# Causal block attention and channel mix on one core: one start-up write moved to ScalarE, and all 1033 tasks in another order

## The chip, the core and the metric

The kernel runs on one core of a Trainium2 chip. The core has five engines that work side by side, each on its own queue of instructions and each strictly in the order of that queue: TensorE (PE, with weight loads shown apart as PEld), VectorE (DVE), ScalarE (ACT), GpSimd (POOL) and SyncE (SP), which here issues every DMA. Engines wait for each other through semaphores. The metric is the device time of one execution in microseconds.

## What is computed

The inputs are q, k and v of 8 batches with 8 heads, 576 positions and 64 numbers per head, and the weights of a channel mix. Attention is causal by blocks of 64 positions:

```python
scores = scale * np.matmul(q, k.transpose(0, 1, 3, 2))
mask = block_i >= block_j                      # position // 64
attn = softmax(np.where(mask, scores, -1e9))
x = np.matmul(attn, v)                         # heads side by side: 512 channels
x_prev = shift of x by one position, zero in front
xk = mu_k * x + (1.0 - mu_k) * x_prev
xr = mu_r * x + (1.0 - mu_r) * x_prev
k = np.maximum(xk @ w_k, 0.0)
v = k * k @ w_v
out = sigmoid(xr @ w_r) * v
```

(The softmax and the shift are written here as words; the rest is the reference.)

## The kernel before

**Tasks and orders.** The kernel first lists its work as 1033 tasks, numbered from 0 in the order in which they are added. Each has a function that issues its instructions, the engines that may do it, and the buffers that it uses from small rings. Nothing is scheduled while it runs: `ORDER` (lines 17 to 72) is a written list of task numbers, and the tasks are issued in that sequence (lines 885 and 886), so the part of the list that falls to one engine is that engine's queue. A word such as `123+1` is task 123 with one fill ahead of it: a matmul of the identity with a width of 512 whose result nobody reads (`unread`, line 257, the matmul is L259). `PLACE` has one letter for each task that more than one engine may do, in order of the numbers: A for ScalarE, D for VectorE, P for GpSimd. A buffer is taken from its ring when the first task that uses it is issued, and freed after the last.

**Stages of one batch.** For batches 0 to 3, long loads bring q and k (tag `ld`, line 234), casts to bfloat16 follow (`long`, L245 on ScalarE, L251 on VectorE and GpSimd), TensorE transposes them (`qt`, L313), and copies put them into `t_qkt` (`ev`). For batches 4 to 7 loads of another layout are cast (`qk`, `tail`) and SyncE transposes them by DMA (`turn`, L377). v is loaded by eight DMAs and cast (`v`). Scores are 12 tasks per batch, `sc b g i` for g of 0 and 1 and i of 0 to 5 (L484), each followed by an exponential on ScalarE, `ex b g i` (L493), which writes `t_e` from the score buffer `t_s` (three in its ring).

Attention outputs come from passes over `t_e`: for batches 1 to 7 an S pass for the row sums (L530, 60 matmuls), a T pass (16), and the value passes A and B (72 each, L541). Batch 0 is done in two parts of its own: positions 0 to 319 and 320 to 575. Each part has column sums (L639) and two value passes (L646). VectorE turns the sums, inverts them and multiplies (t1, rec, t2, norm), which fills columns 1 to 576 of `t_xt`. Column 0 of `t_xt` is the position ahead of the first, and stays zero.

**The mix.** For each of four channel groups a difference of neighbouring columns (`d`, L706, VectorE or GpSimd) and the two mixes (`mul`, L720, VectorE) write `XK` and `XR`. They are worked on in chunks of 512 positions: `pk` multiplies by w_k (L749), `relu` (L760, L762) and `sq` (L770, L772) follow, `pr` multiplies by w_r (L788) with a tanh behind it (L796), `pv` multiplies by w_v (L814), VectorE forms the output (`o`, L826) and SyncE stores it (`store`, L834). `t_mm`, where these products land, has two buffers.

**Task numbers that the text uses.** 100, 101 and 102 are the column sums and the two value passes of the second part of batch 0 (36, 72 and 72 matmuls). 123 and 127 are transposes of batch 1. 165 to 168 are the S, T, A and B passes of batch 1, and 519 to 522 those of batch 6. 543, 547, 551 and 555 are the loads of q and k of batch 7 for heads 0 to 3 and their partners (four DMA commands each); 546, 550, 554 and 558 are the DMA transposes of the same. 563 to 585 (odd) are the scores of batch 7. 966 and above belong to the last two chunks.

Of the kernel before, what the change touches and what calls it, by code (L numbers as in the profile page):

```python
# [11 lines left out]
AF = mybir.ActivationFunctionType  # L12
# [2 lines left out]
LONGS = 4  # L15

ORDER = """
3 0+12 5 4 6 10 7 8 9 11 12 15+8 17 24 16 13 14 18 61+3 63 64 62 19 25 20 21
22 55 57 58 23 56 26 27 28 65 66 29 30 67+1 68 69 70 71+4 33 34 59+2 31 60
32 1 125 72 79+2 82 77 78 81 73 74 83 80 84 85 87 75 126 86 2 127 97 99 121  # L20
76 91 92 122 100 103 98 88 39 41 93 40 123+1 133 124 104 42 134 89 90 94 95
101 102 106 105 107 43 96 108 44 118 115 117 35 116 128 141 119 36 45 46 147
148 143 625 626 129 130 120 142 631 109 632 633 200 112 135 658 136 110 628
659 113 145 629 630 627 37 38 131+1 132 643+4 644 646 144 146 647 648 151
152 649 137 640 645 650 163 164 155 156 652 641 642 651 653 654 655 656 657
153 154 637 638 616 161 162 159 617 201 639 634 635 636 160 139 114 610 611
202 613 203 188 157 140 149 150 158 614 615 660 661 189 190 49 618 111 191
619 612 47 48 138 620 621 50 165 53 166 169 170 168 54 51 622 623 662 52 624
672 196 197 171 172 175 173 198 185 663 192 193 199 673 186 664 194 330 195
167 187 174 228 208 229 176 675 178 177 209 665 676 206 218 216 219 204 222  # L30
669 670 217 223 210 179 343 674 214 215 666 181 211 182 183 180 230 667 231
184 220 221 212 681 699 213 682 224 225 275 226 700 671 693 694 683 227 205
677 678 267 268 207 695 232 679 680 233 236 237 239 238 240 234 241 684 685
686 344 243 271 247 244 696 697 276 277 278 702 272 345 253 698 263 703 245
235 687 264 265 688 689 266 337 701 331 246 704 705 335 690 269 691 692 242
273 274 248 254 257 706 279 710 707 280 270 297 349 250 255 298 711 299 300
256 716 717 258 281 249 259 289 283 336 290 295 708 718 284 296 346 719 709
720 712 293 294 301 303 304 261 302 743 744 745 740 741 291 287 305 288 742
722 723 251 474 737 332 738 713 731 292 714 739 407 732 341 339 306 715 333
285 286 252 725 724 726 728 733 307 282 729 308 311 309 340 312 746 334 747  # L40
668 314 408 338 313 315 734 730 342 748 749 727 310 316 324 398 411 347 735
317 359 736 360 721 262 355 325 413 326 405 750 760 751 761 356 318 367 368
369 319 409 371 320 370 752 753 260 763 764 372 357 348 358 363 364 321 762
757 373 374 351 758 365 352 322 327 328 401 410 790 791 485 754 755 323 366
361 353 362 403 399 778 779 404 329 769 781 770 771 766 350 767 354 375 400
376 379 782 783 380 792 780 382 787 381 793 788 768 789 784 785 383 786 377
412 417 418 765 384 378 385 772 773 389 402 775 776 406 429 421 422 774 423
424 777 390 759 386 387 794 430 414 795 804 805 487 488 391 431 432 439 427
796 388 797 807 395 440 479 397 808 428 806 798 425 799 756 392 426 437 438
433 834 835 393 396 475 801 394 802 816 817 435 434 441 436 419 825 826 810  # L50
420 415 442 416 542 480 446 543 483 811 818 444 476 443 447 448 450 812 449
453 477 451 836 831 478 827 837 459 832 489 481 490 482 484 461 486 460 813
814 815 828 829 553 803 830 819 822 462 820 823 824 557 551 821 445 452 838
839 463 833 842 843 844 464 454 467 501 497 517 498 455 458 502 518 465 456
545 840 468 851 809 457 841 852 503 800 469 507 508 499 500 845 495 544 504
472 491 509 848 846 849 493 878 496 511 880 510 552 879 881 470 549 875 876
555 860 854 492 512 877 513 514 494 547 861 505 515 855 850 856 466 872 857
506 546 516 519 873 858 520 874 548 521 869 870 871 866 867 859 863 523 524
525 868 526 864 865 556 527 522 528 529 862 886 887 558 882 883 530 532 554
579 580 531 583 584 471 550 847 473 573 574 884 885 895 853 581 582 539 541  # L60
567 568 577 578 559 892 896 897 560 893 540 889 894 890 569 565 563 533 922
564 923 561 536 534 537 924 925 919 916 920 917 570 566 538 904 905 921 585
562 575 571 906 901 576 902 586 903 913 914 915 572 926 918 927 587 891 588
590 591 898 899 900 592 593 594 595 910 911 535 907 908 597 607 909 601 888
912 589 596 936 937 928 939 929 608 603 609 938 940 602 933 934 930 931 966
967 941 968 969 970 604 971 598 935 932 599 605 942 948 943 945 949 606 950
951 946 947 944 952 953 954 955 956 960 961 962 957 958 600 1007 963 1008
964 965 1009 959 974 975 976 972 973 983 984 980 981 977 978 979 989 990 992
993 986 991 987 994 988 995 996 985 997 1004 1005 1006 1001 1002 998 999
1010 1011 1012 1013 1014 1015 1000 1003 1021 1022 1024 1025 1016 1017 982  # L70
1023 1030 1026 1031 1032 1018 1027 1019 1020 1028 1029
"""

PLACE = (
    "APAAPAADPPDDPPDDDPAAAAPADDDAPPPPPDPDAAPADDAADADPPDPAPAPADDADDDDPPAAA"
    "AAPAPDDPDDDPDPAPPDDDPDDDPDDPPAPAPPDDDPDPAPPADPDPPPPPDAAAAPPPADPPPPDA"
    "DADDDPAADPAPADAPDPDPDPDPDDDPDDAADPADAPAADPAADAADAAAPAAAPAAAPDPDDAPAD"
    "ADAAAPDAAADPAPDDAAAADAAAAADPDDDPDAAAAADPAAAAAPDDAAADDDDPDPAPADADAPAP"
    "ADADAAADADADAPAPADADAA")


class Plan:
# [53 lines left out]
def kernel(  # L136
# [12 lines left out]
    nc = tc.nc  # L149
# [4 lines left out]
    CCn = C // P  # L154
# [19 lines left out]
    for n, bufs in RINGS.items():  # L174
# [15 lines left out]
    slots = {(ring, at): pools[ring].tile(*SHAPES[ring], tag=f"{ring}{at}",  # L190
                                          name=f"t_{ring}{at}")
             for ring, n in RINGS.items() for at in range(n)}
# [6 lines left out]
    pick = consts.tile([P, 2, QC], F16)  # L199
# [14 lines left out]
            nc.vector.memset(pick[o * D:o * D + D, c,  # L214
                                  u * QC // 2:(u + 1) * QC // 2], 1.0)
    for n in range(RINGS["xt"]):
        nc.vector.memset(slots["xt", n][:, :, 0:1], 0.0)
    if LONGS < B:
        for n in range(RINGS["nl"]):
            nc.gpsimd.memset(slots["nl", n][D:P, :].rearrange(  # L220
# [661 lines left out]
    for (n, cc, a, z), t in mixed.items():  # L882
        t["deps"] += [r for lo, hi, r in readers[n]
                      if lo < z - RT and hi > a - RT]
    for t in plan.order():
        plan.issue(t)


# [28 lines left out]
```

## Time and profile before

| what | value |
|---|---|
| time of the kernel, median of 3 runs | 263.0 us (262.6 to 263.42) |
| the profiled execution, its own time | 261.88 us |
| its span, from the first to the last instruction | 260.1 us |
| mean granted TensorE clock in it | 0.986 |
| fills in the order | 38 |

The span is what the profile's views divide up; 1.78 us lie around it, and the profiled execution was 1.1 us shorter than the median. Times in the views count from the start of the span. A row of the timeline gives start, duration, engine, line, operation, what is written from what, and in brackets how long the engine sat idle before and what ended that. A row of the windows gives the stretch, its length, then busy time and number of instructions of TensorE, its weight loads, VectorE, ScalarE and GpSimd, the granted clock, the busy share of the DMA engines and GB/s. A row of the chain of waits gives start, duration and the piece of work that the end hung on. In the groups by line a row gives the group, its count, busy time, mean duration in ns, and the idle time before it.

### The profile page before, as it was taken

To read this page: it belongs to the slowest core of one execution; us is meant where nothing else is said; L and a number is where in the kernel's file an instruction comes from. 1 tells how busy PE (TensorE), PEld (TensorE's weight loads), DVE (VectorE), ACT (ScalarE), POOL (GpSimd) and SP (SyncE) were. 2 spreads that over 40 slices of the span, in tenths; PEclk is the share of its full clock that TensorE was granted. 3 is DMA by queue.
4 is the path that set the end of the run, shared out by engine and by line. 5 is a ranking of instruction groups with operands and counts; after the bars stand their busy time and mean duration, and the time that the engine had idled before them with its cause. 6 is when DMAs were issued, how large, how long until landed. Compare 5 with 4: busy or idle time off the path is not lost.

```text
span 260.1 us, 8110 instructions
## 1 busy us (share of the span) xinstructions
PE 244.3 (94%) x3434; PEld 124.5 (48%) x3434; DVE 185.4 (71%) x292; ACT 180.9 (70%) x246; POOL 84.6 (33%) x94
## 2 busy tenths in 40 slices
PE   7888379999999999989999999999999999999995
PEld 2545246665466444543554454435534454444442
DVE  0249586999879765796798979786885889543522
ACT  3599849978989998689649667799468840570630
POOL 4423325352255324131540065016351415230110
PEclk9999869999999999999999999999999999999999
DMA  7999999879867799979999899999885202201313
GB/s 224 277 262 359 325 204 312 272 185 222 281 204 176 178 223 226 184 163 229 220 172 260 184 200 159 290 207 226 120 214 156 98 3 81 83 1 40 121 40 124
DMA packets 110132, 48.77 MB, mean 188 GB/s; under 512 B 98704, under 2 KB 98960, under 8 KB 110096
## 3 DMA queue, kind: packets, MB, share of 16 engines
q1 hardware_dynamic: 110096, 48.25, 77.6%
q8 instruction: 27, 0.44, 0.7%
q14 instruction: 9, 0.07, 0.1%
HBM read 33.56 MB, written 9.44 MB: 165 GB/s over the span
## 4 chain that ended last, share of the span: by engine, by line
PE 79%; ACT 5%; DMA 5%; issue 3%; DVE 3%; SPq 2%; POOL 1%; POOLq 0%; ACTq 0%; DVEq 0%
PE t_mm L749 23%; PE t_mm L814 20%; PE t_mm L788 11%; PE t_s L484 7%; PE t_s L541 6%; PE t_s L530 4%; PE t_mm L259 3%; ACT t_e L493 3%; PE t_s L313 2%; SPq L234 2%; DMA t_qkt<-t_nl 2%; DMA t_ld<-in_k_dram 2%; DMA t_vl<-in_v_dram 1%; DVE t_xt L685 1%; PE t_s L646 1%
## 5 line engine op out<-in xcount | busy, mean ns | idle before, releaser
L493 ACT ACTIVATE t_e<-t_s 128x1024 f16<-128x1024 f32 (+3 forms) x96 | 87.7, 975 | 14.6 <-PE t_s L484 14.1
L749 PE MATMUL t_mm<-XK,WK 128*128 128x512 f16 (+2 forms) x320 | 69.6, 363 | 0.8 <-DVE t_o L826 0.6
L814 PE MATMUL t_mm<-WV,t_k 128*128 128x512 f16 (+1 forms) x296 | 66.9, 374 | 0.0
L772 POOL TENSOR_TENSOR t_k<-t_kr 128x512 f16<-128x512 f32 (+2 forms) x31 | 32.1, 1042 | 70.6 <-ACT t_kr L760 38.9
L749 PEld LDWEIGHTS <-WK 128*128 128x128 f16 x320 | 29.5, 99 | 33.4 <-issue 5.1
L826 DVE SCALAR_TENSOR_TENSOR t_o<-t_t,t_mm 128x512 f32<-128x512 f32 (+1 forms) x37 | 24.8, 671 | 28.2 <-PE t_mm L814 20.0
L760 ACT ACTIVATE t_kr<-t_mm 128x512 f32<-128x512 f32 (+2 forms) x50 | 29.1, 583 | 22.2 <-PE t_mm L749 21.6
L814 PEld LDWEIGHTS <-t_k 128*128 128x128 f16 x296 | 28.1, 98 | 33.8 <-issue 2.8
L796 ACT ACTIVATE t_t<-t_mm 128x512 f32<-128x512 f32 x36 | 21.7, 602 | 25.2 <-PE t_mm L788 25.2
L706 POOL TENSOR_TENSOR t_d<-t_xt 128x576 f32<-128x576 f32 (+2 forms) x20 | 21.7, 1091 | 50.6 <-DVE XR L720 19.1
L788 PE MATMUL t_mm<-WR,XR 128*128 128x512 f16 x144 | 36.4, 381 | 0.0
L484 PE MATMUL t_s<-t_qkt 64*64 64x64 bf16 (+7 forms) x672 | 29.7, 288 | 4.2 <-ACT t_e L493 1.4
L720 DVE SCALAR_TENSOR_TENSOR XR<-t_d,MUR,t_xt 128x576 f16<-128x576 f32 (+4 forms) x44 | 31.0, 711 | 0.2
L720 DVE SCALAR_TENSOR_TENSOR XK<-t_d,MUK,t_xt 128x576 f16<-128x576 f32 (+4 forms) x44 | 28.7, 675 | 0.6 <-POOL t_d L706 0.4
L251 POOL CAST t_nl<-t_ld 64x256 bf16<-64x256 f32 (+3 forms) x27 | 22.7, 849 | 16.8 <-DMA t_ld<-in_k_dram 10.2
L484 PEld LDWEIGHTS <-t_qkt 64*64 64x64 bf16 x672 | 14.7, 107 | 21.7 <-issue 16.1
L762 DVE TENSOR_SCALAR t_kr<-t_mm 128x512 f32<-128x512 f32 (+2 forms) x30 | 17.1, 577 | 10.7 <-PE t_mm L749 9.4
L541 PE MATMUL t_s<-t_e,t_vo 64*32 64x64 f16 (+7 forms) x1120 | 20.2, 284 | 0.3 <-POOL t_vo L251 0.3
L772 DVE TENSOR_TENSOR t_k<-t_kr 128x512 f16<-128x512 f32 (+2 forms) x23 | 15.4, 673 | 6.7 <-ACT t_kr L760 6.3
L788 PEld LDWEIGHTS <-XR 128*128 128x128 f16 x144 | 12.5, 98 | 15.4 <-issue 3.8
L541 PEld LDWEIGHTS <-t_vo 64*32 64x32 f16 x1120 | 14.5, 93 | 7.7 <-issue 2.5
L597 DVE TENSOR_TENSOR t_xt<-t_s,t_rt 128x1024 f32<-128x1024 f32 x14 | 16.9, 1218 | 0.7 <-PE t_s L541 0.6
(49 smaller groups left out, 188.6 us busy)
## 6 DMA issues: line engine op xcount, KB each, us to landing
t_vl<-in_v_dram SPq DMA_DIRECT2D x64, 144.0 KB, 3.7
out_dram<-t_o SPq DMA_DIRECT2D x35, 256.0 KB, 2.8
t_ld<-in_q_dram SPq DMA_DIRECT2D x16, 288.0 KB, 4.6
t_ld<-in_k_dram SPq DMA_DIRECT2D x16, 288.0 KB, 4.7
t_ld<-in_q_dram SPq DMA_DIRECT2D x36, 128.0 KB, 3.4
t_ld<-in_k_dram SPq DMA_DIRECT2D x36, 128.0 KB, 3.4
t_ld<-in_moe_w_k_dram SPq DMA_DIRECT2D x4, 512.0 KB, 7.0
t_ld<-in_moe_w_v_dram SPq DMA_DIRECT2D x4, 512.0 KB, 6.8
```

The source lines that it names most:

```text
L251: e.tensor_copy(dst, src)
L484: nc.tensor.matmul(PS[o * D:o * D + D, y, col:col + n], kq[:, 1, t * D:t * D + D], kq[:, 0, q0:q0 + n], start=True, stop=True)
L493: nc.scalar.activation(new(ebuf)[:, :, 0:w], new(m)[:, :, 0:w], AF.Exp, scale=ISQ)
L541: nc.tensor.matmul(PA[out_, u, HALF + f * D:HALF + f * D + D] if kind == "T" else PA[out_, u, lo - D:lo - D + n], weight(b, u, c, t % JT, ...
L706: (nc.vector if eng == "DVE" else nc.gpsimd).tensor_tensor(dt[:, lo:hi], x[:, cc, 1 + lo:1 + hi], x[:, cc, lo:hi], ALU.subtract)
L720: nc.vector.scalar_tensor_tensor((XK, XR)[n][:, cc, pos:pos + w], new(d)[:, at:at + w], (MUK1, MUR1)[n][:, cc:cc + 1], x, ALU.mult, ALU.add)
L749: nc.tensor.matmul(ps, WK[:, cc, jc * P:(jc + 1) * P], XK[:, cc, t0 % RT:t0 % RT + w], start=(cc == 0), stop=(cc == CCn - 1))
L760: nc.scalar.activation(kt, ps, AF.Relu)
L772: (nc.vector if eng == "DVE" else nc.gpsimd).tensor_tensor(dst, KR, KR, ALU.mult)
L788: nc.tensor.matmul(ps, XR[:, cc, t0 % RT:t0 % RT + P], WR[:, cc], start=(cc == 0), stop=(cc == CCn - 1))
L814: nc.tensor.matmul(ps[:, 0:w], k2[:, jc, jt * P:(jt + 1) * P], WV[:, jc, cols], start=(jc == 0), stop=(jc == JCn - 1))
L826: nc.vector.scalar_tensor_tensor(new(o)[:, 0:w], new(tiles["tbf", c, jt])[:, cols], 1.0, new(m)[:, 0:w], ALU.add, ALU.mult)
```

## The change

There are three edits. Column 0 of the two `t_xt` buffers is zeroed by ScalarE (a copy of part of `pick`, times 0) in place of VectorE, still ahead of all tasks; it is then the first operation of ScalarE. `ORDER` is another sequence of the same 1033 tasks, with 56 fills in place of 38, and `PLACE` gives some tasks to other engines. The loop that issues the tasks now notes what each one issued, with a condition that ends in `and 0`, so its dependency is never added. The computation is the same.

Of the two lists the rows are shown on which the text draws.

```diff
--- before
+++ after
 ORDER = """
-3 0+12 5 4 6 10 7 8 9 11 12 15+8 17 24 16 13 14 18 61+3 63 64 62 19 25 20 21
-22 55 57 58 23 56 26 27 28 65 66 29 30 67+1 68 69 70 71+4 33 34 59+2 31 60
...
-76 91 92 122 100 103 98 88 39 41 93 40 123+1 133 124 104 42 134 89 90 94 95
-101 102 106 105 107 43 96 108 44 118 115 117 35 116 128 141 119 36 45 46 147
...
-420 415 442 416 542 480 446 543 483 811 818 444 476 443 447 448 450 812 449
...
-814 815 828 829 553 803 830 819 822 462 820 823 824 557 551 821 445 452 838
...
-555 860 854 492 512 877 513 514 494 547 861 505 515 855 850 856 466 872 857
-506 546 516 519 873 858 520 874 548 521 869 870 871 866 867 859 863 523 524
-525 868 526 864 865 556 527 522 528 529 862 886 887 558 882 883 530 532 554
-579 580 531 583 584 471 550 847 473 573 574 884 885 895 853 581 582 539 541
...
-562 575 571 906 901 576 902 586 903 913 914 915 572 926 918 927 587 891 588
...
-1023 1030 1026 1031 1032 1018 1027 1019 1020 1028 1029
+3 0+12 5 4 8 9 6 10 17 19 18 12 7 24 25 11 13+9 15 16 14 59+5 60 63 57 26 20
...
+122 86 65 88 89 90 41 42 97 94 95 66 102+5 43 44 128 123+2 100+5 124 39 40
+45 103 98 104 35 622 96 36 101 623 145 99 141 129 130 624 146 46 37 105 625
...
+827 845 490 517 452 839 454 846 506 499 463 464 467 555 553 466 507 508 847
...
+864 865 880 881 551 495 494 496 511 515 471 860 861 862 866 872 873 512 516
+520 519 552 867 543 868 869 870 456 547 854 855 523 524 856 871 544 875 857
+850 526 858 525 522 529 521 874 528 554 876 877 527 557 558 533 859 892 893
+579 580 473 853 577 546 575 576 539 541 578 534 884 885 886 548 549 550 571
+569 894 585 572 586 559 895 844 887 540 570 888 924 535 583 896 925 573 581
...
+1026 1022 1023 1030 1031 1018 1032 1027 1019 1020 1028 1029...
 """
 PLACE = (
-    "APAAPAADPPDDPPDDDPAAAAPADDDAPPPPPDPDAAPADDAADADPPDPAPAPADDADDDDPPAAA"
...
+    "PDDDDADAPPADPDDDPDAAAPAPADAADPDDDDPDAAPAAADDDPDDPDPAPDPAPADADPDDPAAA"
...
     for n in range(RINGS["xt"]):
-        nc.vector.memset(slots["xt", n][:, :, 0:1], 0.0)
+        nc.scalar.activation(slots["xt", n][:, :, 0], pick[:, 0, 0:CCn],
+                             AF.Copy, scale=0.0)
...
+    shared = ("long", "qk", "tail", "v", "w", "d", "mul", "sq")
+    ahead = None
     for t in plan.order():
+        n0 = len(nc.cur_bb.bb.instructions)
         plan.issue(t)
+        made = nc.cur_bb.bb.instructions[n0:]
+        if t["eng"] == "DVE" and t["key"].split()[0] in shared:
+            ahead = made[-1]
+        elif t["eng"] == "POOL" and ahead is not None and 0:
+            tc.add_manual_dep(
+                made[0], ahead.name, mybir.DependencyInfo(
+                    mybir.DependencyClass.Sync,
+                    mybir.DependencyReason.DATA), reason="turns")
```

Read from the letters and the lists, the tasks move between engines like this (before, after):

| task | ScalarE | VectorE | GpSimd |
|---|---|---|---|
| squares | 26, 27 | 23, 28 | 31, 25 |
| relu | 50, 52 | 30, 28 | |
| differences | | 16, 22 | 20, 14 |
| casts of q and k (long, qk, tail) | 15, 16 | 10, 13 | 27, 23 |
| casts of v | 3, 1 | 8, 6 | 5, 9 |
| casts of weights | 6, 7 | 3, 1 | 1, 2 |
| copies of transposes | 13, 12 | 7, 8 | |

## What was predicted

> **What bounds the kernel now.** I read the page first: busy time, granted clock, and the chain that ended last.
>
> ```profile
> PE 244.3 (94%) x3434; PEld 124.5 (48%) x3434; DVE 185.4 (71%) x292; ACT 180.9 (70%) x246; POOL 84.6 (33%) x94
> PEclk9999869999999999999999999999999999999999
> PE 79%; ACT 5%; DMA 5%; issue 3%; DVE 3%; SPq 2%; POOL 1%; POOLq 0%; ACTq 0%; DVEq 0%
> ```
>
> TensorE is busy in 94% of the span of 260.1 us. A new order can win only the other 15.8 us (260.1 - 244.3) and the time lost at a lower clock, and the clock row dips in one place alone, near 30 us. So next I read the waits of TensorE and the timeline there.
>
> ```profile
> PE t_s L646 <- issue: 4.8, 2, 4.0
> 26.50 1.54 PEld L646 LDWEIGHTS <-t_vo 64*32 64x32 f16 x128 [1.09 <-issue]
> 26.50 1.70 PE L646 MATMUL t_s<-t_e,t_vo 64*32 64x256 f16 x128 [0.81 <-issue]
> 32.15 0.23 PE L646 MATMUL t_s<-t_e,t_vo 64*32 64x64 f16 x1 [3.95 <-issue]
> 34.28 1.07 PE L484 MATMUL t_s<-t_qkt 64*64 64x384 bf16 x12 [1.33 <-DVE t_xt L685]
> q8 instruction: 27, 0.44, 0.7%
> ```
>
> In the value passes of batch 0 TensorE stops twice for "issue": 0.81 us, then 3.95 us. Between the stops lie exactly 128 matmuls and 128 weight loads, 256 instructions. The instruction queue q8 moved 27 packets, 0.44 MB / 27 = 16 KB each, and 6868 TensorE instructions / 27 = 254. So I read both stops as TensorE waiting for its next block of 256 instructions. It took those 256 in 1.70 us, and the next block could run only 32.15 - 26.50 = 5.65 us after the start of the one before. After that comes a wait of 1.33 us for VectorE, itself late by the stop, and the clock:
>
> ```profile
> 30.00:31.00 1.00, 0.00 (x0) 0.00 (x0) 0.00 (x0) 1.00 (x2) 0.00 (x0) 0.86 0.98 364
> 32.00:34.00 2.00, 0.81 (x5) 0.28 (x6) 1.53 (x3) 0.00 (x0) 0.75 (x1) 0.50 0.93 269
> 34.00:36.00 2.00, 1.72 (x15) 0.85 (x15) 1.84 (x5) 0.98 (x2) 0.47 (x2) 0.50 1.22 185
> 36.00:37.00 1.00, 1.00 (x5) 0.60 (x4) 0.43 (x2) 0.95 (x2) 0.34 (x1) 0.50 0.90 176
> 37.00:38.00 1.00, 1.00 (x13) 0.77 (x12) 1.00 (x3) 0.37 (x1) 0.00 (x0) 0.73 0.98 184
> ```
>
> The clock is halved to about 37.5 us. TensorE was busy 0.81 + 1.72 + 1.00 + 0.54 = 4.1 us of that time, so about half, 2.0 us, was lost. Without the block stops TensorE would gain at most 0.81 + 3.95 + 1.33 + 2.0 = 8.1 us.
>
> But another engine stands close behind. I cut the span at the first exponential of batch 0 (11.76) and the last of batch 1 (51.51).
>
> ```profile
> 11.76:51.51 39.75, 31.55 (x627) 19.99 (x629) 29.25 (x58) 33.91 (x40) 13.60 (x18) 0.91 0.98 286
> 51.51:257.00 205.49, 203.14 (x2758) 100.03 (x2750) 154.60 (x227) 142.43 (x201) 65.19 (x60) 1.00 0.74 165
> 35.02 1.94 ACT L493 ACTIVATE t_e<-t_s 128x1024 f16<-128x1024 f32 x2 [3.53 <-PE t_s L484]
> 37.63 0.44 ACT L760 ACTIVATE t_kr<-t_mm 128x320 f32<-128x320 f32 x1 [0.68 <-PE t_mm L749]
> ```
>
> In the first stretch ScalarE is the fuller one: 33.91 us busy against TensorE's 31.55. It is idle for 5.84 us there, and 3.53 + 0.68 = 4.21 us of these are the stop seen from ScalarE. After 51.51 TensorE sits idle for 205.49 - 203.14 = 2.35 us only, so little is left to win.
>
> **The change, part by part.** *The block stops.* Before, the two value passes of the second part of batch 0 (tasks 101 and 102, 72 matmuls each) stand next to each other. In the new order 77 matmuls of task 102 (5 of them fills) are followed by 11 (2 fills), 41 (5 fills) and 4 others before 101. I cut the new TensorE stream into the same blocks.
>
> ```profile
> 23.04 1.15 PE L639 MATMUL t_mm<-t_e,pick 128*32 128x256 f16 x36
> 40.20 0.50 PE t_s L313 x9
> 48.12 0.54 PE t_mm L749 x4
> ```
>
> One edge falls after matmul 56 of task 102, the next after matmul 51 of task 101: 21 + 11 + 41 + 4 + 51 = 128. That is 72 value matmuls at 1.70 / 128 = 0.013 (1.0 us), nine transposes (0.5), 36 column sums (1.15), four of L749 (0.54) and seven fills at 0.24 (1.7, row below): 4.9 us in place of 1.70. The block before it comes to 4.5 us in the same way. Against the 5.65 us above, stops of 1.1 and 0.8 us remain. I take these 1.9 us, of which 0.9 us reaches ScalarE through the transposes of batch 1 behind the first; bounds are 0 and the old 4.76 us (0.81 + 3.95). When the clock fell, TensorE had been idle from 28.20 (32.15 - 3.95) to about 30.7 (the 0.86 of the row at 30), 2.5 us; stops of 1 us are far shorter, so the half clock goes.
>
> [...]
>
> *ScalarE's work in the first stretch.* Counted from the two orders and the engine letters, between those exponentials ScalarE has 45 operations in place of 39.
>
> ```profile
> L760 ACT ACTIVATE t_kr<-t_mm 128x320 f32<-128x320 f32 x3 | 1.3, 440 | 0.7 <-PE t_mm L749 0.7
> L770 ACT ACTIVATE t_k<-t_kr 128x320 f16<-128x320 f32 x3 | 1.5, 505 | 0.0
> L245 ACT COPY t_qkt<-t_mm 128x512 bf16<-128x512 bf16 x2 | 1.4, 725 | 2.7 <-PE t_mm L313 2.7
> L245 ACT CAST WK<-t_ld 128x1024 f16<-128x1024 f32 x4 | 4.2, 1054 | 0.0
> L245 ACT CAST t_vo<-t_vl 128x1152 f16<-128x1152 f32 x3 | 3.5, 1161 | 0.0
> ```
>
> Added: three relu (about 0.4 us each, two sizes), four squares (0.5 and less), one copy of 0.73; removed: one weight cast of 1.05, one value cast of 1.16. Sum +1.2 + 1.9 + 0.7 - 1.05 - 1.16 = +1.6 us. Operations overlap their neighbours by about 0.1 us, so six more give +1.0 us on the path. Bounds 0 and 1.6.
>
> *Fills and start.* Fills rise from 38 to 56.
>
> ```profile
> 1.37 5.30 PE L259 MATMUL t_mm<-identb 128*128 128x512 bf16 x12 [1.37 <-POOL identb masks.py:199]
> 3.67 1.28 ACT L245 ACT_TABLE_LOAD   x1 [3.67 <-DMA t_ld<-in_q_dram]
> 7.83 1.89 PE L259 MATMUL t_mm<-identb 128*128 128x512 bf16 x8 [0.53 <-ACT t_qkt L245]
> 11.09 0.63 PE L484 MATMUL t_s<-t_qkt 64*64 64x256 bf16 x16 [0.22 <-ACT t_qkt L245]
> ```
>
> One costs 1.89 / 8 = 0.24 us. Ahead of the first scores stand 9 and 5 in place of 8 and 3: 3 x 0.24 = 0.7 us, less the waits that PE has there anyway (0.22 is shown): I take +0.4 us, bounds 0 and 0.7. The other 15 stand where TensorE waits for ScalarE: nothing, and at worst 15 x 0.24 = 3.6 us. The zero columns pull the table load of 1.28 us out of the stretch from 3.67 us on. Nothing starts earlier by it: the 12 cold fills hold TensorE until 6.67 in both, and ScalarE now takes neither half of q. Saved 0, at most 1.28. The new operation waits for VectorE's fill of `pick`, and nothing queued behind it has data yet. The block with `and 0` makes no dependency.
>
> So the first stretch ends earlier by 4.21 - 0.9 - 1.0 - 0.4 = 1.9 us. TensorE's own account gives as much or more (8.1 - 1.9 - 0.7 - 3.6 = 1.9 with every fill paid, 5.5 with the other 15 free), so ScalarE decides.
>
> *The rest of the order.* VectorE takes over four full squares and two full differences from GpSimd.
>
> ```profile
> L772 DVE TENSOR_TENSOR t_k<-t_kr 128x512 f16<-128x512 f32 x19 | 13.6, 723 | 6.7 <-ACT t_kr L760 6.3
> L706 DVE TENSOR_TENSOR t_d<-t_xt 128x576 f32<-128x576 f32 x14 | 10.5, 754 | 0.2
> 173.22 1.18 SPq L234 DMA_DIRECT2D t_ld<-in_q_dram  x2
> 176.72 1.12 SPq L234 DMA_DIRECT2D t_ld<-in_k_dram  x2
> 178.52 9.68 SPq L377 DMA_TRANSPOSE t_qkt<-t_nl  x4
> 180.13 1.36 PE t_s L530 x60
> PE t_s L484 <- DMA t_qkt<-t_nl: 0.6, 1, 0.6
> 190.92 0.33 PE t_s L484 x4
> 256.91 0.42 DVE t_o L826
> ```
>
> 4 x 0.723 + 2 x 0.754 = 4.4 us more VectorE work, covered by its 51 us of idle time after 51.51 (205.49 - 154.60). The last tasks after the final scores are the same kinds in nearly the same sequence, with the last VectorE operation at 256.91: 0. The idle 2.35 us may grow, because TensorE comes 1.9 us earlier to loads whose queue does not go faster; before, it waited 0.6 us for batch 7's transposes. I take +0.4 us, bounds -2.35 and +4.5 (rival B).
>
> Sum: -1.9 + 0.4 = -1.5 us. From the span of 260.1 that is 258.6, from the profiled execution's 261.88 it is 260.4. That execution lies 1.1 us under the median of 263.0, so the forecast is 263.0 - 1.5 = 261.5 us.
>
> **The rivals.** A, *TensorE was the true limit early.* ScalarE's idle time may close up too, since fills and spread passes keep it fed; then up to 5.5 us come back: 263.0 - 5.5 = 257.5, typically 259. For it: 5.84 us of ScalarE idle time; against it: 45 operations.
>
> B, *SyncE's queue becomes the wait of batch 7 (slower).* Before, the last q and k loads of batch 7 were issued by 177.84, ahead of batch 6's S pass at 180.13. In the new order the last two pairs, eight commands, stand behind that pass: 8 x 0.56 (1.12 / 2) = 4.5 us, with four transposes at 9.68 / 4 = 2.4 us still to follow. If SyncE isn't ahead of TensorE there, the first scores of batch 7 wait up to 4.5 us: 263.0 - 1.9 + 4.5 = 265.6, some 264.8 with a part hidden. It decides once SyncE's lead is under about 2 us; it was 180.13 - 177.84 = 2.3 us.
>
> C, *the stop isn't the fetch of a block, or a block still stops as long*: the 4.76 us and the half clock stay, and the extra ScalarE work and fills come on top: 263.0 + 1.0 + 0.4 = 264.4 us. The 256 between the stops speak against it.
>
> D, *the gain is eaten*: remaining stops and fills cost what the stop did: 262.2 to 263.8.
>
> **How the numbers follow.** A measurement of this kernel can tell about 0.3% (0.8 us) from no change, so faster means under 262.2 and slower over 263.8. The forecast's case (260 to 262.2) has 0.40, A 0.16, D 0.20, B 0.18, C 0.06. That is faster 0.56, same 0.20, slower 0.24. The range from 258.6 to 265.2 cuts off the far half of A and the worst of B, about 0.15 together; the likeliest case's own range is 260.0 to 262.2.
>
> **What would show it.** Right: no idle time of TensorE above 1.5 us before "issue" on L646, a clock row without a dip after the first slice, 45 ScalarE operations in some 37 us, batch 1's S pass near 49.5 us. Wrong: a clock dip elsewhere, or TensorE waiting over 2 us for t_qkt near 188 us, which is B.

## The result, and the profile after

The changed kernel takes **264.59 us** (median of 20 runs, 262.14 to 266.08), the kernel before 262.98 us (20 runs, 260.40 to 264.28). The ratio is 1.0058, with an interval of 1.0036 to 1.0080: slower by 0.6%. The forecast was 261.5 us, faster by 0.6%. The range held the time, the direction was wrong.

The profiled execution of the changed kernel took 263.02 us with a span of 261.2, 1.6 us under its median; that of before lay 1.1 us under its own. So the two traces show 1.1 us of the 1.6 us difference. First the page of the changed kernel: busy time, granted clock, and the chain that ended last.

```profile
PE 247.8 (95%) x3452; PEld 125.0 (48%) x3452; DVE 195.2 (75%) x299; ACT 179.0 (69%) x250; POOL 78.3 (30%) x83
PEclk9999999999999999999999999999999999999999
PE 76%; DMA 8%; SPq 5%; DVE 4%; ACT 4%; issue 1%; POOL 1%; POOLq 0%; DVEq 0%; ACTq 0%
```

The clock row has lost its dip and "issue" has fallen from 3% of the chain to 1%: what the new order was to take away is gone. But DMA and SyncE's queue (SPq) have gone from 5% and 2% of the chain to 8% and 5%. SPq's rise lies early: ahead of the first product with w_v the chain runs along SyncE's queue from 33.15 to 45.6 us. In the DMA share, three transposes of q and k stand on the chain where there was one (start and duration; before, then after):

```profile
185.65 5.22 DMA t_qkt<-t_nl
```

```profile
111.07 4.83 DMA t_qkt<-t_nl
132.74 5.45 DMA t_qkt<-t_nl
162.50 4.05 DMA t_qkt<-t_nl
```

To see what that is worth, cut both spans at the same point, TensorE's S pass of batch 1 (task 165), which started at 51.17 us before and at 49.02 us after. Columns are the cut, its length, then busy time of TensorE, its weight loads, VectorE, ScalarE and GpSimd, granted clock, DMA share and GB/s. First the windows of the kernel before, then those of the changed one.

```profile
11.76:51.17 39.41, 31.21 (x611) 19.66 (x609) 28.91 (x57) 33.57 (x39) 13.60 (x18) 0.91 0.98 285
51.17:256.91 205.74, 203.48 (x2767) 100.35 (x2766) 154.85 (x228) 142.77 (x202) 65.19 (x60) 1.00 0.75 166
```

```profile
11.13:49.02 37.89, 33.47 (x629) 19.91 (x620) 28.68 (x59) 34.58 (x45) 11.71 (x13) 1.00 0.93 271
49.02:258.01 208.99, 205.31 (x2772) 100.80 (x2771) 162.26 (x230) 141.35 (x201) 62.32 (x56) 1.00 0.75 169
```

The S pass comes 2.15 us earlier (51.17 - 49.02), where 1.9 us were forecast. Of these, 1.52 us are the stretch itself (39.41 - 37.89). The other 0.63 us lie ahead of the first exponential (11.76 and 11.13), and the order doesn't explain them: the 12 opening fills, the same in both orders, took 5.30 us before and 4.33 us here.

```profile
1.37 4.33 PE t_mm L260 x12
```

In the traces of the experiments below these fills took 4.07 to 5.30 us, 4.13 us in one with the old start. The earlier S pass itself holds: it came at 51.2 to 53.2 us in every trace with the old start and at 48.4 to 50.8 us in every one with the new start.

The rest is **3.25 us longer** (208.99 - 205.74). TensorE's idle time there grew by 1.42 us (3.68 instead of 2.26) and its busy time by 1.83 us. The groups of TensorE's instructions in that window show which (busy time of the group, mean of one, idle time before it and what ended that; the busy times count overlaps twice). Before, then after:

```profile
L484 PE MATMUL t_s<-t_qkt 64*64 64x64 bf16 (+7 forms) x480 | 20.7, 289 | 1.3 <-ACT t_e L493 0.7 <-DMA t_qkt<-t_nl 0.6
L541 PE MATMUL t_s<-t_e,t_vo 64*32 64x64 f16 (+7 forms) x1120 | 20.2, 284 | 0.3 <-POOL t_vo L251 0.3
L313 PE MATMUL t_s<-identb,t_nl 128*128 128x128 bf16 x54 | 3.8, 220 | 0.0
```

```profile
L485 PE MATMUL t_s<-t_qkt 64*64 64x512 bf16 (+7 forms) x480 | 21.7, 289 | 2.5 <-DMA t_qkt<-t_nl 2.4
L542 PE MATMUL t_s<-t_e,t_vo 64*32 64x64 f16 (+7 forms) x1120 | 20.6, 284 | 0.0
L314 PE MATMUL t_s<-identb,t_nl 128*128 128x128 bf16 x63 | 4.5, 219 | 0.0
L815 PE MATMUL t_mm<-WV,t_k 128*128 128x512 f16 (+1 forms) x296 | 67.3, 374 | 0.6 <-ACT WV L248 0.6
```

The scores wait 1.8 us longer for the transposed q and k (2.4 instead of 0.6 us), while waits of 0.7 us for ScalarE and 0.3 us for v have gone, and the same 480 score matmuls are busy for 1.0 us longer. Nine more transposes stand behind the cut, 0.7 us that were only moved there from the first stretch. The value passes add 0.4 us, and 0.6 us are waited for the first block of w_v. On TensorE's timeline the waits for q and k look so:

```profile
114.89 0.33 PE L485 MATMUL t_s<-t_qkt 64*64 64x256 bf16 x8
115.94 0.63 PE L485 MATMUL t_s<-t_qkt 64*64 64x448 bf16 x16 [0.72 <-DMA t_qkt<-t_nl]
136.83 0.32 PE L485 MATMUL t_s<-t_qkt 64*64 64x320 bf16 x2
138.23 0.54 PE L485 MATMUL t_s<-t_qkt 64*64 64x320 bf16 x14 [1.07 <-DMA t_qkt<-t_nl]
165.70 0.30 PE L485 MATMUL t_s<-t_qkt 64*64 64x256 bf16 x2
166.59 0.77 PE L485 MATMUL t_s<-t_qkt 64*64 64x256 bf16 x18 [0.60 <-DMA t_qkt<-t_nl]
```

Each time a score pass starts, gets through a few matmuls, and stops until one more transposed block lands: once each in batches 4, 5 and 6. Now SyncE's queue ahead of them, whose DMA_TRANSPOSE are the turns; other rows of it are left out. First the kernel before:

```profile
117.59 1.75 SPq L377 DMA_TRANSPOSE t_qkt<-t_nl  x1
128.89 3.05 SPq L377 DMA_TRANSPOSE t_qkt<-t_nl  x2
154.80 7.41 SPq L377 DMA_TRANSPOSE t_qkt<-t_nl  x4
```

Then the changed kernel:

```profile
99.36 1.08 SPq L235 DMA_DIRECT2D t_ld<-in_k_dram  x2
104.35 1.44 SPq L378 DMA_TRANSPOSE t_qkt<-t_nl  x1
125.51 1.18 SPq L235 DMA_DIRECT2D t_ld<-in_k_dram  x2
130.52 1.37 SPq L378 DMA_TRANSPOSE t_qkt<-t_nl  x1
132.74 5.61 SPq L378 DMA_TRANSPOSE t_qkt<-t_nl  x3
154.96 2.96 SPq L378 DMA_TRANSPOSE t_qkt<-t_nl  x2
157.97 0.68 SPq L835 DMA_DIRECT2D out_dram<-t_o  x1
158.81 1.35 SPq L378 DMA_TRANSPOSE t_qkt<-t_nl  x1
160.27 2.12 SPq L835 DMA_DIRECT2D out_dram<-t_o  x2
162.50 1.44 SPq L378 DMA_TRANSPOSE t_qkt<-t_nl  x1
```

Read the gaps. After 100.44 us (99.36 + 1.08) SyncE does nothing for 3.9 us, and after 126.69 us (125.51 + 1.18) nothing for 3.8 us: the turn at the head of its queue waits for a cast, and all behind it waits too. For batch 5, before, one of four turns was issued at 117.59 and the others from 128.89 on; now all four come from 130.52 on. For batch 6, before, the four turns stood together; now three stores stand among them, two of these (2.12 us) ahead of the last. The casts themselves stand late on their engines: the one for the turn at 130.52 us ended at 130.37 us (129.72 + 0.65) on VectorE, though its load had been issued by 119.15 us (117.96 + 1.19).

### The profile page after: what moved, and what is told of

The parts are those of the page before. It is cut to its first block, busy times and chain, and to the rows that moved or that the text cites. A ratio compares the mean times of both kernels' runs of the same rounds, so it can differ in the third digit from the quotient of the medians.

```text
span 261.2 us, 8144 instructions
## 1 busy us (share of the span) xinstructions
PE 247.8 (95%) x3452; PEld 125.0 (48%) x3452; DVE 195.2 (75%) x299; ACT 179.0 (69%) x250; POOL 78.3 (30%) x83
## 4 chain that ended last, share of the span: by engine, by line
PE 76%; DMA 8%; SPq 5%; DVE 4%; ACT 4%; issue 1%; POOL 1%; POOLq 0%; DVEq 0%; ACTq 0%
PE t_mm L815 22%; PE t_mm L750 21%; PE t_mm L789 10%; PE t_s L485 7%; DMA t_qkt<-t_nl 5%; PE t_s L542 5%; SPq L235 5%; PE t_s L531 3%; PE t_mm L260 3%; ACT t_e L494 2%; DMA t_ld<-in_moe_w_v_dram 2%; PE t_s L260 2%; PE t_s L314 2%; DVE XK L721 1%; PE t_s L647 1%
## 5 line engine op out<-in xcount | busy, mean ns | idle before, releaser
L494 ACT ACTIVATE t_e<-t_s 128x1024 f16<-128x1024 f32 (+2 forms) x96 | 87.9, 977 | 17.5 <-PE t_s L485 17.0
L761 ACT ACTIVATE t_kr<-t_mm 128x512 f32<-128x512 f32 (+2 forms) x52 | 29.8, 575 | 23.7 <-PE t_mm L750 23.1
L750 PEld LDWEIGHTS <-WK 128*128 128x128 f16 x320 | 28.6, 97 | 31.6 <-issue 5.1
L773 POOL TENSOR_TENSOR t_k<-t_kr 128x512 f16<-128x512 f32 (+2 forms) x25 | 26.6, 1067 | 55.4 <-DVE t_kr L763 38.8
L721 DVE SCALAR_TENSOR_TENSOR XK<-t_d,MUK,t_xt 128x576 f16<-128x576 f32 (+4 forms) x44 | 33.4, 776 | 1.7 <-POOL t_d L707 1.4
L707 POOL TENSOR_TENSOR t_d<-t_xt 128x576 f32<-128x576 f32 (+2 forms) x14 | 16.2, 1161 | 50.5 <-DVE XR L721 16.9
L721 DVE SCALAR_TENSOR_TENSOR XR<-t_d,MUR,t_xt 128x576 f16<-128x576 f32 (+4 forms) x44 | 29.4, 679 | 1.4 <-POOL t_d L707 1.3
L252 POOL CAST t_nl<-t_ld 128x1152 bf16<-128x1152 f32 (+3 forms) x23 | 21.2, 934 | 27.4 <-DMA t_ld<-in_q_dram 19.0
L773 DVE TENSOR_TENSOR t_k<-t_kr 128x512 f16<-128x512 f32 (+1 forms) x28 | 19.9, 730 | 12.2 <-ACT t_kr L761 11.9
L763 DVE TENSOR_SCALAR t_kr<-t_mm 128x512 f32<-128x512 f32 (+2 forms) x28 | 16.3, 586 | 7.2 <-PE t_mm L750 6.4
```

The costliest lines, as they stand in the source:

```text
L252: e.tensor_copy(dst, src)
L494: nc.scalar.activation(new(ebuf)[:, :, 0:w], new(m)[:, :, 0:w], AF.Exp, scale=ISQ)
L721: nc.vector.scalar_tensor_tensor((XK, XR)[n][:, cc, pos:pos + w], new(d)[:, at:at + w], (MUK1, MUR1)[n][:, cc:cc + 1], x, ALU.mult, ALU.add)
L750: nc.tensor.matmul(ps, WK[:, cc, jc * P:(jc + 1) * P], XK[:, cc, t0 % RT:t0 % RT + w], start=(cc == 0), stop=(cc == CCn - 1))
L761: nc.scalar.activation(kt, ps, AF.Relu)
L773: (nc.vector if eng == "DVE" else nc.gpsimd).tensor_tensor(dst, KR, KR, ALU.mult)
```

## The experiments

Ratios are to the kernel before, on the same chip (its medians there: 262.95 to 263.51 us). The two orders differ in the place of nearly every task, so I first separated the parts.

**The zero columns.** The kernel before with the new zero write, and the changed kernel with the old one:

```diff
-        nc.vector.memset(slots["xt", n][:, :, 0:1], 0.0)
+        nc.scalar.activation(slots["xt", n][:, :, 0], pick[:, 0, 0:CCn],
+                             AF.Copy, scale=0.0)
```

> The old order with the new zero write on ScalarE alone. Theory (the table load is hidden behind the first 12 fills): no change, within 0.3 us of before. Rival (ScalarE's first cast of q sets the start): up to 1.28 us faster. In the profile the table load should stand before 3.67 us.

> The new order with the old zero write on VectorE. Theory (the zero write is worth nothing here): as the changed kernel, some 1.5 us slower than before, within 0.4 us. Rival (the new order needs ScalarE free of the table load at 7 us): 1 us slower than the changed kernel. Second rival (the zero write itself does harm): back at before's time.

Measured: 0.9992 (0.9944 to 1.0041) for the first, 1.0088 (1.0057 to 1.0119) for the second. The loss comes with the order: it is there without the new write, and the write doesn't bring it to the old order. In the old order the write is worth nothing within 0.6%. The new order without it measured 0.3% (0.8 us) above the changed kernel's 1.0058, with intervals that overlap, so a small gain of the write there isn't excluded.

**The fills and the block stops.** The old order with 18 more fills in the value pass of batch 0 at which TensorE stopped longest (the fills write the buffer of the pass before, so a part of batch 0's attention output is changed), and the new order without its 44 fills behind the first 12:

```diff
-95 101 102 106 105
+95 101 102+18 106 105
```

> The old order with 18 fills ahead of task 102, the second of the two adjoining value passes. Theory (the stop is the fetch of a block; fills lengthen the block of 1.70 us by 18 x 0.22 = 3.9 us): the long stop shrinks from 4 us to under 1 us, the fills take its place at no cost, the clock no longer falls, and the kernel gains what the half clock cost on the path: 1 to 2 us, 261 to 262. Rival 1 (ScalarE sets the start, so the clock's loss is hidden): within 0.5 us of before. Rival 2 (the stop isn't the fetch): it stays and the fills add 3.9 us.

```diff
-25 11 13+9 15 16 14 59+5 60 63
+25 11 13 15 16 14 59 60 63
...
-95 66 102+5 43 44 128 123+2 100+5 124 39
+95 66 102 43 44 128 123 100 124 39
...
```

> The new order without the 44 later fills; the 12 at the start stay. Theory (fills stand where TensorE waits): the same fetch stops and waits come back as idle time, TensorE's idle time rises by 5 us or more in the first 35 us, the clock may fall there; 0 to 3 us slower than the changed kernel. Rival (fills are paid): up to 44 x 0.22 = 9.7 us, at least 2 us, faster than the changed kernel.

Measured: 0.9974 (0.9943 to 1.0005) and 1.0057 (1.0028 to 1.0087). With the fills the 3.95 us stop is gone from the old order (the third row is the 18 fills, as they stand on the chain of that run):

```profile
PE t_s L644 <- issue: 1.6, 1, 1.6
11.70:52.21 40.51, 35.11 (x633) 21.38 (x629) 27.99 (x57) 33.28 (x39) 13.64 (x18) 0.96 0.94 279
28.65 5.20 PE t_s L257 x18
```

One stop of 1.6 us is left, at the edge ahead of the fills (0.81 us in the kernel before), so a longer block took the stop at its end away. But the fills took 5.20 us, more than the 3.95 us stop that they replace. ScalarE waited for the scores behind them for 5.7 us, where it had waited for 3.53 us, and the S pass of batch 1 came at 52.21 us, not earlier than the 51.17 us of before. So this run shows that the stop can be taken away, and not what the start is worth without it. Without fills the new order runs at half clock for a while, and it hardly matters:

```profile
11.10:49.46 38.36, 32.49 (x611) 21.61 (x609) 29.22 (x59) 34.45 (x45) 11.67 (x13) 0.79 0.97 279
10.40:24.00 13.60, 11.45 (x224) 8.04 (x225) 7.04 (x14) 11.91 (x14) 3.84 (x5) 0.50 0.99 257
```

TensorE ran 13.6 us at half clock, the mean clock of the first stretch fell to 0.79, and the S pass came at 49.46 us, 0.4 us behind the 49.02 us of the changed kernel. So TensorE's speed didn't set this part of the new order. ScalarE's busy time (34.45 and 34.58 us) is the same, and it is the fullest engine there. That it sets the stretch is not shown: in the changed kernel it is idle for 3.3 us of it (37.89 - 34.58), and the DMA engines are busy for 0.93 of it.

**Halves.** Four kernels took one order up to a task and the other from there on. The cut, in the list of the first and third kernel, where the new order goes over into the old one:

```diff
 620 148 660 52 165
-645 166 661 169 48 170 172
+633 645 201 114 202 203 661
```

```diff
 668 201 202 178 168
-208 182 203 184 175 267 183
+203 662 672 175 185 663 673
```

> The new order and engines up to and with the S pass of batch 1, then what is left in the old order with the old engines. Theory A (start and rest are independent: the new start gains 2.1 us, the new rest loses 3.3 to 3.7): 2.1 us faster than before, 260.9. Rival B (the loss comes from arriving earlier at loads whose queue is not faster): the 2.1 us are given back, within 0.5 us of before.

> The old order and engines up to and with the S pass of batch 1, then what is left in the new order with the new engines. Theory A (independent): 3.3 to 3.7 us slower than before, 266.3 to 266.7. Rival B (the new rest only loses because TensorE reaches it earlier): as the changed kernel or better, 263 to 264.6.

> New order and engines up to and with the first value pass of batch 1's second half (task 168), the old order and engines from there on; one step further than the first half-and-half, so that no load or cast is left behind the cut. Theory: the new start is worth what the two traces show at batch 1's score pass (51.17 us before, 49.02 after, some 2.1 us; at this cut about 1.4 us), and the loss comes from the rest of the new order. Then about 261.6 us, ratio about 0.995. Rival: the rest loses because it is reached earlier than its loads land, whatever its order; then the old rest loses the gain as well and the ratio is 1.000 or above.

> The counterpart: old order and engines up to and with the first value pass of batch 1's first half (task 167), the new order and engines from there on. From the same amount of TensorE work done, the old rest took 196.4 us (60.43 to 256.87) and the new one 199.0 us (59.0 to 258.0). Theory: the new rest costs this 2.6 us whatever stands before it: about 265.6 us, ratio about 1.010. Rival: reached later, its loads are there in time and it costs what the old one does: about 263 us, ratio about 1.000.

Measured: 1.0222 (1.0161 to 1.0283), 1.0264 (1.0215 to 1.0313), 1.0143 (1.0103 to 1.0183), 1.0221 (1.0177 to 1.0266). All four lost, three of them more than either theory allowed (for the third the rival had said 1.000 or above), and the traces show the seams. In the first:

```profile
57.48 2.10 PE L312 MATMUL t_s<-identb,t_nl 128*128 128x128 bf16 x18 [6.60 <-DVE t_nl L250]
56.10:62.90 6.80, 5.13 (x107) 3.60 (x108) 5.26 (x8) 2.08 (x2) 0.00 (x0) 0.50 0.95 205
```

A load that the new order makes early and the old one late had fallen behind the cut: 6.6 us of waiting, then 6.8 us at half clock. The third kernel has no such load behind its cut, reached the S pass at 48.39 us, and lost it again in five waits of 0.4 to 0.6 us at the scores of batch 2, 3.4 us at half clock and, at 187 us, a new stop at the edge of a block:

```profile
186.85 2.58 PE L748 MATMUL t_mm<-XK,WK 128*128 128x512 f16 x11 [1.58 <-issue]
```

So the times of these four say only that the two orders don't join at these places without a loss. Their traces say more, for the waits for q and k come with one half alone. Here they are in the second and in the fourth kernel, which have the old start and the new rest (in total, times, longest):

```profile
PE t_s L482 <- DMA t_qkt<-t_nl: 2.4, 3, 1.2
PE t_s L482 <- DMA t_qkt<-t_nl: 2.0, 3, 0.9
```

They stand at the scores of batches 4, 5 and 6 again, though the second kernel began its S pass of batch 1 at 53.20 us, 2.0 us later than the kernel before. The first and the third, with the new start and the old rest, have no such wait. So these waits belong to the new order of the rest, and not to reaching it earlier.

**Single waits.** So I left the new order whole and moved single tasks. First the turns of batches 5 and 6 (n3_early_turns in the expectations): the casts that they wait for stand earlier on VectorE (400) and ScalarE (477), and the stores (800, 809) behind the last turn (490).

```diff
-415 370 788 413
+415 370 400 788 413
...
-379 479 400 781 782
+379 479 781 782
...
-435 444 432 814
+435 444 477 432 814
...
-816 812 477 478 482
+816 812 478 482
...
-451 453 809 826 459 800 462 460 461 488 824 827 845 490 517
+451 453 826 459 462 460 461 488 490 800 809 824 827 845 517
```

> The new order with four moves that let SyncE issue the DMA transposes of batches 5 and 6 earlier: the cast qk of batch 5's first pair ahead of three VectorE tasks, batch 6's tail cast ahead of an exponential, and two stores behind the last transpose of batch 6. Theory (the new order gives part of the gain back because TensorE waits for those transposes): TensorE's waits of 1.1 us near 138 us and 0.6 us near 167 us go, and the kernel is 1 to 1.7 us faster than the changed one, 263 to 263.6. Rival (TensorE would wait for the next thing anyway): within 0.4 us of the changed kernel.

Measured: 262.42 us, 0.9976 (0.9942 to 1.0011). Against the changed kernel's 1.0058 that is 0.8%, 2.1 us, more than the 1 to 1.7 us expected (at the least 0.25%, between the near ends of the intervals). SyncE was idle for 0.2 us ahead of batch 5's turns in place of 3.8 us. Of the three waits for q and k this one is left, in batch 4:

```profile
118.73 0.63 PE L483 MATMUL t_s<-t_qkt 64*64 64x448 bf16 x16 [1.03 <-DMA t_qkt<-t_nl]
L483 PE MATMUL t_s<-t_qkt 64*64 64x512 bf16 (+7 forms) x480 | 21.1, 289 | 1.1 <-DMA t_qkt<-t_nl 1.0
```

The busy time of the score matmuls went from 21.7 to 21.1 us as well: it fits that a stop inside a pass also costs busy time (ahead of the stop in batch 6, two matmuls took 0.30 us; behind it, 18 took 0.77 us). The gain of 2.1 us doesn't show in this trace, whose execution was 1.1 us over its median, where that of the changed kernel was 1.6 us under its own. The rest behind the S pass takes 209.0 us in both: TensorE waited for w_v for 1.46 us in place of 0.60, and for 1.14 us at the transposes after it. The wait for w_v varies by itself: it was 1.70 us in the trace of the changed kernel with the old zero write.

Then the wait for w_v, by issuing its last two loads, the first block's among them, ahead of batch 1's second v:

```diff
-639 142 139 157
+639 142 51 47 139 157
...
-617 618 51 194 615 150 159 47 196 644
+617 618 194 615 150 159 196 644
```

> The new order with the last two loads of w_v issued ahead of the second half of batch 1's v load, 23 places earlier. Theory (TensorE waits for the cast of w_v at its first product with w_v, 0.6 us in the profile and 1.7 us in another run): the wait goes, 0.6 to 1.5 us faster than the changed kernel. Rival (the v load behind it comes late instead, or ScalarE is the next to be late): within 0.4 us of the changed kernel.

Measured: 265.45 us, 1.0087 (1.0053 to 1.0121): no gain. The wait for w_v has gone, and two others have come:

```profile
51.91 1.46 PE L540 MATMUL t_s<-t_e,t_vo 64*32 64x64 f16 x84 [1.13 <-POOL t_vo L250]
55.04 0.68 PE L312 MATMUL t_s<-identb,t_nl 128*128 128x128 bf16 x9 [1.67 <-POOL t_nl L250]
```

The loads that were put back are the next ones late. Next, the shape of tiles on TensorE. In the two traces a 64-row matmul starts 0.31 us after a 128-row one, where a second 128-row one starts after 0.22 us (medians), so I put this change at about 0.1 us, an estimate. The new order changes between 64 and 128 rows 120 times in place of 108, and in batches 2 to 7 the T pass no longer stands directly behind the S pass. Put back there:

```diff
-233 232 281 236
+232 233 281 236
...
-444 477 432 814 811 443 816 812
+477 432 814 811 443 444 816 812
...
```

> The new order with its turns early (as in n3_early_turns), and in batches 2 to 7 the small pass behind the score pass directly behind it, as in the old order, so that the tile shape on TensorE changes less often. Theory: each change costs some 0.1 us, so 0.5 to 0.9 us less than n3_early_turns: 261.5 to 262.0 us, ratio 0.994 to 0.996 to the kernel before. Rival: the extra busy time of the new order isn't from the changes; then within 0.3 us of n3_early_turns, ratio 0.997 to 0.999.

Measured: 262.82 us, 0.9985 (0.9953 to 1.0018), the rival's value; one of its 12 executions took 1376.88 us and isn't in the ratio. But the edit doesn't do what it was meant to do: by the list, TensorE now changes between 64 and 128 rows 124 times, and 120 times without it. So the price of a change stays untested.

Then, on top of n3_early_turns, ready work in front of the waits that were left, on SyncE and on TensorE (n6_filled_waits):

```diff
-411 252 334 718
+411 252 342 334 718
...
-346 732 342 733 309
+346 732 733 309
...
-330 177 669 114
+330 177 168 669 114
...
-202 178 168 208 182
+202 178 664 662 208 182
...
-207 671 664 665 662 185
+207 671 665 185
```

> The new order with its turns early (as in n3_early_turns) and two more waits taken away by moving ready work in front of them: the turn of batch 4's block 2, whose inputs are written 8 us earlier, ahead of that of block 0 on SyncE's queue, and on TensorE batch 1's last value pass (task 168) ahead of the first product with w_v, and the two r products 664 and 662 ahead of batch 2's first scores. Theory: what is left of the loss against the start's gain is waits of TensorE for single late inputs; n3_early_turns still had 1.46 us at w_v, 1.14 at the transposes after it and 1.03 at batch 4's scores, and a third to a half of the first two may come back elsewhere. Then 1.5 to 2.5 us less than n3_early_turns: about 260.4 us, ratio about 0.990, below both kernels. Rival: TensorE in this stretch is paced by the loads, so that a wait filled in one place opens in another, as with the early loads of w_v; then only batch 4's 0.7 to 1.0 us are gained: about 261.6 us, ratio about 0.995.

Measured: 264.02 us, 1.0019 (0.9981 to 1.0057), worse than both theories. The wait in batch 4 was gone, but batch 1's last value pass, moved ahead of w_v, brought two stops:

```profile
54.50 0.81 PE L540 MATMUL t_s<-t_e,t_vo 64*32 64x512 f16 x23 [1.55 <-DVE t_xt L588]
57.13 0.92 PE L540 MATMUL t_s<-t_e,t_vo 64*32 64x448 f16 x49 [1.82 <-issue]
58.60:62.00 3.40, 3.40 (x16) 1.84 (x15) 0.69 (x1) 0.01 (x1) 0.81 (x1) 0.50 0.67 150
```

The first ended with VectorE's normalization of the other half, which had to be through first. The second is the stop of the kernel before, made anew: two value passes of 72 small matmuls come close to each other, and by the count of TensorE's instructions the edge of a block of 256 falls at 57.1 us, where TensorE stops for 1.82 us in the middle of the pass; 3.4 us at half clock follow. So the last run took the edit on SyncE alone, the first four lines of the diff above, on top of n3_early_turns.

> Of the edits of n6_filled_waits only the one on SyncE: batch 4's turn of block 2 ahead of that of block 0, the rest as in n3_early_turns. In the trace of n6_filled_waits the wait at batch 4's scores (1.03 us in n3_early_turns) is gone, while the two moves on TensorE before 60 us brought two new waits (1.55 and 1.82 us) and 3.4 us at half clock. Theory: the two are independent, and the turn alone is worth the wait that it removes: 0.7 to 1.0 us less than n3_early_turns, 261.4 to 261.7 us, ratio 0.993 to 0.995, below both kernels. Rival: after batch 4 something else is late by as much (VectorE's mixes for the k products, which waited 0.53 us in each run): as n3_early_turns, 262.4 us, ratio 0.998.

Measured: **260.44 us, 0.9873 (0.9831 to 0.9914)**, faster than both kernels, and by more than expected. Its windows, its score matmuls, and SyncE's queue, where the turn of block 2 now fills the gap in front of block 0's:

```profile
11.20:50.84 39.64, 35.19 (x640) 21.52 (x638) 28.92 (x59) 34.34 (x46) 11.75 (x13) 0.96 0.92 268
50.84:257.40 206.56, 204.79 (x2772) 100.50 (x2771) 162.72 (x231) 141.12 (x201) 62.61 (x56) 1.00 0.76 169
L483 PE MATMUL t_s<-t_qkt 64*64 64x512 bf16 (+7 forms) x480 | 20.9, 289 | 0.1
102.66 5.47 SPq L376 DMA_TRANSPOSE t_qkt<-t_nl  x2
```

The rest behind the S pass takes 206.56 us, 2.4 us less than in the changed kernel, with no wait for q and k. It is within 0.8 us of the kernel before, of which the nine moved transposes are 0.7. This profiled execution (262.32 us) was the slowest of its six and had the lowest granted clock (0.993, the others 0.999 to 1.000): the clock dips in its first stretch (0.96), and the S pass came at 50.84 us.

## Why the prediction was wrong

- **The block stops and the half clock: right.** The clock row has no dip, and the stops left for "issue" on L647 are 0.8 us in all, where 1.1 and 0.8 us were forecast. Such a stop could be taken away (by 18 fills in the old order) and made anew (by the value pass moved ahead of w_v). Rival C falls. TensorE doesn't stop at every edge: in the third of the halves 384 matmuls, three blocks' worth, lie between two stops (32.40 and 56.33 us). Where it stopped, it stood for up to 3.95 us in the kernel before, and for 1.82 and 1.58 us in two experiments.
- **The first stretch: right in its time, in part by luck.** ScalarE's 45 operations came with 1.0 us more work (34.58 in place of 33.57 us), as forecast. Its idle time fell by 2.5 us (from 5.84 to 3.31), where 3.3 us were forecast (4.21 - 0.9). The first exponential came 0.63 us earlier, with the opening fills, where 0.4 us later was forecast. These two errors nearly cancel, so 2.15 us against 1.9 says less than it seems. The step's ground, that ScalarE decides there, stays open. Rival A did not come: 3.3 us of ScalarE's idle time are left, and half clock for 13.6 us moved the end of the stretch by 0.4 us.
- **Fills and zero columns: nearly right.** For the fills 0.4 us were forecast; without them the new order takes the same time (1.0057 and 1.0058). The zero columns were put at 0, and in the old order they are, within 0.6%.
- **"The rest of the order", +0.4 us: this step failed.** It measured +3.25 us, inside its bounds of -2.35 to +4.5, and it turned the sign. The step expected a wait only because TensorE would come earlier to loads whose queue goes no faster. So it looked at batch 7, where the loads stand behind the S pass, found 2.3 us of lead there, and gave the case 0.18; in the changed kernel TensorE doesn't wait for q and k in batch 7 at all. What came in its place are waits in batches 4, 5 and 6 that the new order makes itself: with the old start, which reaches the rest later than the new one does, they come too (2.4 and 2.0 us). The turns of these batches weren't compared between the two lists: which cast each waits for, where this cast stands on its engine, and which stores are queued between them. All of that stands in the two lists. Rival B named the right queue and the right tile, but the wrong place and the wrong reason.
- **How much of the loss this is.** Two casts, two stores and two turns moved took the kernel from 1.0058 to 0.9976 and 0.9873. From the changed kernel to the last that is 1.2% at the least, between the near ends of their intervals (1.0036 - 0.9914), and no less than the 1.1% of waits for q and k and of longer scores that the two traces show ((1.8 + 1.0) / 263). So the turns are enough to explain the whole loss. The last of these runs brought 1.0% by the ratios, and at the least 0.3% (0.9942 - 0.9914), where its wait was 1.03 us (0.4%); whether it is worth more than its wait stays open. Loads and stores behind a turn on SyncE come earlier with it as well, but this wasn't tried by itself.
- **Not the cause, and open.** The wait for w_v only moves. The price of a change of tile shape isn't settled; behind the S pass there are only four more such changes (84 in place of 80), 0.4 us at some 0.1 us each as an estimate.

With six tasks moved so that its turns come early, the new order is faster than the kernel before by 1.3% (0.9 to 1.7%), where the forecast had 0.6%; a part of that may be that its turns now come better than those of the kernel before, which had 0.6 us of such waits itself.

## What to carry to other kernels

When an order is planned anew, compare for each in-order queue what stands at its head and what it waits for, in every repetition of the loop: one late cast in front of a transfer holds all transfers behind it (3.8 and 3.9 us of SyncE's time here), and such waits can cost as much as a stop of the bottleneck engine that took far more work to remove (2.4 us at the scores, against the 2.15 us that the new start won). Six moved tasks decided here whether the new plan of all the others lost 0.6% or won 1.3%. And judge a new plan by its stretches, from one common point on: a gain of 2.15 us and a loss of 3.25 us look like a change that does nothing. Read more than one trace for it: the 12 opening fills alone differ by 1.2 us between traces (4.07 to 5.30).

## What the runs showed of the hardware

- The stops for "issue" lie 128 matmuls, with as many weight loads, or a multiple of that apart: 128 in the kernel before (26.50 to 32.15 us), 384 in the new order without fills (28.50 to 52.84 us), 1152 in the third of the halves (108.20 to 186.85 us). Such a stop isn't tied to batch 0, nor is the time between two edges fixed: TensorE stopped for 1.82 us in batch 1 with 6.5 us from edge to edge, and for 1.58 us near 187 us with 4.3 (182.59 to 186.85), where the kernel before had 5.65 and stopped for 3.95 us.
- In these runs the clock was granted at half for multiples of some 3.4 us: 3.4 (58.6 to 62.0 us in n6_filled_waits), 6.8 in the kernel before (30.7 to 37.5 us) and in the first of the halves behind the wait of 6.6 us, 13.6 without the fills. In the kernel before the clock fell when TensorE had been idle for 2.5 us. So long a stop isn't needed: in the third of the halves it fell at 69.0 us after four waits of 0.44 to 0.58 us in the 3.6 us before.
- A stop inside a pass seems to cost busy time too: the same 480 score matmuls behind the S pass took 21.7 us with 2.4 us of waits for q and k, 21.1 us with 1.0 us, and 20.9 us without. So a larger busy time may come from a wait; how much of it does isn't separated from other causes.
